# Seeding a PSUM bank with a ScalarE copy instead of summing two products on VectorE

## The chip, the cores and the metric

The kernel runs on one core of a Trainium2 chip. The metric is the device time of one execution in microseconds; the time before is 638.24 us, the median of three runs (637.68 to 638.25). Of one execution there is a profile, whose span is 636.4 us.

## The reference

The reference chains two blocks. The first is a state-space scan ("mamba2"): for 4 sequences of 768 tokens with 8 heads it works in chunks and gives, per token, 8 x 32 = 256 numbers. The second is a mixture of four experts over the resulting 3072 x 256 matrix:

```python
p = domain_probs / (domain_probs.sum(-1, keepdims=True) + 1e-09)
for e in range(E):
    h = np.maximum(x @ w1[e], 0.0)          # 256 -> 1024
    out += p[:, e:e + 1] * (h @ w2[e])      # 1024 -> 256
```

Everything is float32. The change concerns only the first product of an expert and its gate: `h = max(x @ w1, 0)`, scaled by the token's probability p.

## The kernel before

**Tiling.** The tokens come in 6 blocks of 512 (index k). For each block the kernel runs 8 steps (index r): 4 experts times 2 parts of the hidden layer. The steps are numbered n = 8k + r, from 0 to 47. Steps 0 and 1 are done plainly; steps 2 to 47 go through the loop at L820, and the change concerns only these.

**Seven products instead of eight.** In a step, both matrix products are done as 2 x 2 blocks by a Strassen-Winograd scheme: seven block products, of weights and tokens that were added up beforehand, take the place of eight. `fmul(n, i)`, L509 to L525, is the i-th product of the first layer: two matmul instructions of 128 x 256 in the program, each of which shows as two matmul records and two weight loads in the profile. `smul(n, i)`, L593 to L611, is the i-th product of the second layer, of the same size; it adds into the accumulators acc0 to acc3. In step n the loop mixes the `fmul` of step n with the `smul` of step n - 1, so that TensorE has work while VectorE and ScalarE prepare the hidden values of step n.

**Two banks of PSUM, X and Y.** The first layer's products go to two banks. X takes products 1, 6, 7 and 4, one added on the other. Y takes product 2 alone, and is then started again for products 5 and 3. The four blocks of the hidden layer are sums of these:

- block 11 = product 1 + product 2
- block 22 = products 1 + 6 + 7, plus product 5
- block 12 = products 1 + 6, plus products 5 + 3
- block 21 = products 1 + 6 + 7 + 4, which is X at the end

For the first three, X is needed at an intermediate stage. `snap(n, i)`, L527 to L530, is a ScalarE copy of X to SBUF after product i. `total(n, i, b)`, L532 to L535, is a VectorE sum of Y and that snapshot into a tile z. `gated(n, b, src)`, L537 to L547, is the VectorE instruction that takes the maximum with zero, multiplies by the gate p and writes the hidden block h; its source is z, or X for block 21. `diff`, L549 to L552, subtracts hidden blocks for the second layer.

**Order.** The schedule is written out by hand: each engine runs its instructions in the order of the program's text, and the framework only adds the semaphore waits. A step before the change begins so on TensorE: fmul 1 (X), fmul 2 (Y), smul(n-1, 1), fmul 6 (X), smul(n-1, 3), fmul 5 (Y), fmul 7 (X). On ScalarE it is snapshot 1, snapshot 6, snapshot 7; on VectorE it is the sum and the gate of block 11, then two late differences and attention work of the step before (`late`, `decay_part`, `combine`), then the sum and gate of block 22, and so on. Some steps also hold attention work: `masks` (ScalarE), `scores` (TensorE, steps with r = 3 and 6) and `outputs` (TensorE, r = 4 and 7). The scores of such a step borrow the banks X and Y at its end, and VectorE's masked products (L405) free them. `opened(n)`, L715 to L719, is the head of a step. `leave` issues the stores of a finished block on the DMA queue of SyncE.

**What waits on what, around the change.** fmul 6 adds to X, so it may run only after the snapshot of product 1 has been taken. fmul 5 restarts Y, so it may run only after the reader of product 2 in Y is done. A matmul with `start` set replaces what is in its bank; without it, it adds to what is there.

Of the kernel before, what the change touches and what calls it, by code (L numbers as in the profile page):

```python
# [8 lines left out]
FP32 = mybir.dt.float32  # L9
# [3 lines left out]
P = 128  # L13
# [4 lines left out]
def kernel(  # L18
# [38 lines left out]
    nc = tc.nc  # L57
# [6 lines left out]
    HB = BLK // 2  # L64
    CPB = BLK // P
# [6 lines left out]
    JJ = FH // HB  # L72
# [17 lines left out]
    ps_f = ctx.enter_context(tc.tile_pool(name="ps_f", bufs=1, space=bass.MemoryType.PSUM))  # L90
# [126 lines left out]
    for queue, c in ((nc.sync, slice(0, 1)), (nc.scalar, slice(1, SPREAD))):  # L217
        queue.dma_start(
            out=a_q.rearrange("(q r) c t s -> q r c (t s)", q=NQ)[:, 0, c],
            in_=a.rearrange("(i k) (q t) s -> k q i (t s)", k=NBLK, t=NT)[0][:, c])  # L220
# [4 lines left out]
        out=a_sb, in_=a.rearrange("c h s -> (c h) s").rearrange("(p r) s -> p r s", r=2))  # L225
# [147 lines left out]
    def masks(c):  # L373

        s = st[c]
        m = s["ctm"] = att.tile([HN, NT, P], FP32, tag="ctm", name="ctm")
        for t in range(NT):
            nc.scalar.mul(m[:, t], s["xb"][:, OCT:OCT + P], tmask[:, t:t + 1])
# [128 lines left out]
    first, hid, acc = {}, {}, {}  # L507

    def fmul(n, i):  # L509

        k = n // SPB
        f = first.setdefault(n, {})
        bank = "X" if i in (1, 6, 7, 4) else "Y"
        if i in (1, 2, 5):
            f[bank] = ps_f.tile([P, JJ, HB], FP32, tag=bank, name=bank)
        y, Y = yT[k], yS.get(k)
        w = (A11, A12, S4, A22, S1, S2, S3)[i - 1]
        b1, b2 = slice(0, HB), slice(HB, BLK)
        rhs = {1: y[:, 0, b1], 2: y[:, 1, b1], 3: y[:, 1, b2]}.get(i)
        if rhs is None:  # L520
            rhs = Y[:, {4: 3, 5: 0, 6: 1, 7: 2}[i]]
        for j in range(JJ):
            nc.tensor.matmul(  # L523
                out=f[bank][:, j], lhsT=wt1[n][:, w, j * P:j * P + P], rhs=rhs,
                start=(i in (1, 2, 5) and j == 0), stop=(j == JJ - 1), skip_group_check=True)  # L525

    def snap(n, i):  # L527

        s = first[n][i] = ffn.tile([P, JJ, HB], FP32, tag="snap", name="snap", bufs=4)
        nc.scalar.copy(out=s, in_=first[n]["X"])  # L530

    def total(n, i, b):  # L532

        z = first[n]["z" + b] = ffn.tile([P, JJ, HB], FP32, tag="z", name="z", bufs=3)
        nc.vector.tensor_add(z, first[n]["Y"], first[n][i])  # L535

    def gated(n, b, src):  # L537

        if n not in hid:
            hid[n] = {}  # L540
        h = hid[n][b] = ffn.tile([P, JJ, HB], FP32, tag="h" + b, name="h" + b)
        k, e = n // SPB, n % SPB // JJ
        half = int(b[1]) - 1
        g = gate[k, e].rearrange("p c s -> p (c s)")[:, half * HB:half * HB + HB]
        nc.vector.scalar_tensor_tensor(  # L545
            out=h, in0=first[n][src], scalar=0.0, in1=g.unsqueeze(1).to_broadcast([P, JJ, HB]),
            op0=ALU.max, op1=ALU.mult)  # L547
# [33 lines left out]
    def plain_second(n, b, d):  # L581


        k = n // SPB
        u, half = {(1, 1): (2, 1), (2, 1): (3, 0), (1, 2): (0, 1), (2, 2): (3, 1)}[d, b]
        begins = begin(k, u)
        for i, w in enumerate(((A11, A12), (S3, A22))[d - 1]):
            for j in range(JJ):
                nc.tensor.matmul(  # L589
                    out=acc[k, u][:, half], lhsT=w2_op(n, w)[:, j], rhs=hid[n][f"{i + 1}{b}"][:, j],  # L590
                    start=(begins and i == 0 and j == 0), stop=False, skip_group_check=True)

    def smul(n, i):  # L593

        if n < 0:
            return
        k = n // SPB
        if n < PLAIN:
            if n == PLAIN - 1 and i in (1, 7, 6, 4):
                m, d = divmod((1, 7, 6, 4).index(i), 2)  # L600
                plain_second(m, 2, d + 1)
            return
        u, half = divmod(ORDER.index(i), 2)
        begins = begin(k, u)
        w = (A11, A12, S4, A22, S1, S2, S3)[i - 1]
        rhs = hid[n][("11", "21", "22", "T4", "T1", "T2", "T3")[i - 1]]
        for j in range(JJ):
            nc.tensor.matmul(  # L608
                out=acc[k, u][:, half], lhsT=w2_op(n, w)[:, j], rhs=rhs[:, j],
                start=(begins and j == 0),  # L610
                stop=(n % SPB == SPB - 1 and j == JJ - 1), skip_group_check=True)  # L611
# [97 lines left out]
    def leave(k, c):  # L709

        for q in range(P // 32):
            for d in range(2):
                leave_part(k, c, q, d, nc.sync)

    def opened(n):  # L715

        fmul(n, 1)
        snap(n, 1)
        fmul(n, 2)  # L719


    homes = ((ps_s, "acc0"), (ps_s, "acc1"), (ps_att, "att"), (ps_att, "att"))
# [97 lines left out]
    for n in range(PLAIN, NS):  # L820
        k, r = divmod(n, SPB)

        ahead = CPB * (k + 1)
        scanned = [ahead + d for d in {0: [0], 2: [1], 4: [2], 5: [3]}.get(r, [])]
        scored = [ahead + d for d in {3: [0, 1], 6: [2, 3]}.get(r, [])]
        done = [ahead + d for d in {4: [0, 1], 7: [2, 3]}.get(r, [])]
        if k == NBLK - 1:
            scanned, scored, done = [], [], []
        ending = r == 0 and k > 0
        e = r // JJ  # L830
        if r % JJ == 0 and n + JJ < NS:
            load_gate(*divmod(n // JJ + 1, E))
        if PLAIN + 2 < n + 2 < NS:
            load_w1(n + 2)
            load_w2(n + 2)
        opened(n)
        total(n, 1, "11")
        gated(n, "11", "z11")
        behind = scored and k == 0
        last = behind and r == 6  # L840
        for work in late[:2] if behind else late:
            work()
        if r == 1 and k > 0:
            combine(k - 1, 0)
            combine(k - 1, 1)
        for c in scanned:
            decay_part(c, 0)
        for c in scored:
            masks(c)
        if k > 0 and 2 <= r < CPB + 2:  # L850
            leave(k - 1, r - 2)
        smul(n - 1, 1)
        fmul(n, 6)
        snap(n, 6)
        smul(n - 1, 3)
        if ending:
            keep(k - 1, 0)
        if done:
            outputs(done)
            states.extend(done)  # L860
        fmul(n, 5)
        fmul(n, 7)
        snap(n, 7)
        total(n, 7, "22")
        smul(n - 1, 7)
        smul(n - 1, 5)
        if ending:
            keep(k - 1, 1)
        gated(n, "22", "z22")
        if r == 1 and k > 0:  # L870
            combine(k - 1, 2)
        for c in scanned:
            decay_part(c, 1)
        for work in late[2:] if behind and not last else []:
            work()
        for c in scored if not last else []:
            decay_part(c, 2)
        if n == PLAIN:
            sum_w2(0, 1)
        elif n == SPB - 4:  # L880
            sum_w1(n + 2)
        elif n >= SPB - 3:
            sum_w2(n)
        if n < CPB:
            load_chunk(n + CPB)
        for c in scanned if n >= CPB else []:
            if c + 2 < NCH:
                load_decays(c + 2)
        for c in done:
            if c + CPB < NCH:  # L890
                load_tokens(c + CPB)
                load_heads(c + CPB)
        fmul(n, 3)
        total(n, 6, "12")
        fmul(n, 4)
        gated(n, "21", "X")
        for work in late[2:] if last else []:
            work()
        for c in scored if last else []:
            decay_part(c, 2)  # L900
        if not scored:
            gated(n, "12", "z12")
        if r == SPB - 1 and k < NBLK - 1:
            sums(k + 1)
        smul(n - 1, 6)
        if scored:
            scores(scored, ((ps_att, "att"), (ps_att, "att"), (ps_f, "Y"), (ps_f, "X")))
            masked(scored, (3, 2, 0, 1))
            gated(n, "12", "z12")
        smul(n - 1, 2)  # L910
        diff(n, "T3", "22", "12")
        smul(n - 1, 4)
        if n == PLAIN:
            sum_w2(1, 1)
        if n != SPB - 4:
            sum_w1(n + 2)
        if PLAIN < n < SPB - 4:
            sum_w2(n + 1)
        diff(n, "T1", "12", "11")
        if r == 1 and k > 0:  # L920
            turned_out(k - 1)
        late = [lambda n=n: diff(n, "T2", "22", "T1"), lambda n=n: diff(n, "T4", "21", "T2")]
        if states:
            late.append(lambda c=states.pop(0): carry(c))
# [48 lines left out]
```

## Time and profile before

| what | before |
|---|---|
| time, median of 3 runs | 638.24 us |
| span of the profiled execution | 636.4 us |
| TensorE busy | 631.9 us |
| VectorE busy | 483.4 us |
| ScalarE busy | 119.7 us |
| snapshots of X (L530) | 138, 586 ns each |
| sums of Y and a snapshot (L535) | 138, 686 ns each |
| gates that read z (L545) | 138, 724 ns each |
| gates that read X (L545) | 50, 684 ns each |

In the profile, PE is TensorE's matmul, PEld its weight load, DVE is VectorE, ACT is ScalarE and POOL is GpSimd. A row of the groups reads: line, engine, operation, output and input tile, shape, count, then the busy time and the mean of one in ns, then the idle time of the engine just ahead of these instructions and what ended it. A row of the timeline reads: start in us, length in us, engine, line, operation, count, and in brackets the idle time before it and what ended that. Matmul records overlap, so the length of a group of them is longer than the time it takes from the next one.

### The profile page before, as it was taken

To read this page: it belongs to the slowest core of one execution; us is meant where nothing else is said; L and a number is where in the kernel's file an instruction comes from. 1 tells how busy PE (TensorE), PEld (TensorE's weight loads), DVE (VectorE), ACT (ScalarE), POOL (GpSimd) and SP (SyncE) were. 2 spreads that over 40 slices of the span, in tenths; PEclk is the share of its full clock that TensorE was granted. 3 is DMA by queue.
4 is the path that set the end of the run, shared out by engine and by line. 5 is a ranking of instruction groups with operands and counts; after the bars stand their busy time and mean duration, and the time that the engine had idled before them with its cause. 6 is when DMAs were issued, how large, how long until landed. Compare 5 with 4: busy or idle time off the path is not lost.

```text
span 636.4 us, 9259 instructions
## 1 busy us (share of the span) xinstructions
PE 631.9 (99%) x3405; PEld 538.2 (85%) x3405; DVE 483.4 (76%) x810; ACT 119.7 (19%) x264; POOL 112.9 (18%) x164
## 2 busy tenths in 40 slices
PE   9999999999999999999999999999999999999997
PEld 5888888888888888888888888888888888888886
DVE  7868999887787788678687778778867677756555
ACT  4011221212111221122211221122111211111110
POOL 6788557020000002000002000000100000100001
PEclk9999999999999999999999999999999999999999
DMA  6998894745666392757284566639365644167001
GB/s 188 302 357 295 282 346 156 279 169 166 191 200 238 90 366 81 228 175 248 99 287 149 168 199 196 231 102 358 89 220 162 242 160 133 61 152 241 2 1 33
DMA packets 98513, 121.61 MB, mean 191 GB/s; under 512 B 29529, under 2 KB 81957, under 8 KB 98469
## 3 DMA queue, kind: packets, MB, share of 16 engines
q1 hardware_dynamic: 95512, 111.20, 53.7%
q0 software_dynamic: 2432, 9.50, 3.8%
q8 instruction: 27, 0.44, 0.3%
q10 hardware_dynamic: 524, 0.32, 0.2%
q14 instruction: 18, 0.14, 0.1%
HBM read 108.16 MB, written 12.83 MB: 190 GB/s over the span
## 4 chain that ended last, share of the span: by engine, by line
PE 99%; ACT 0%; DVE 0%; issue 0%
PE acc L608 44%; PE X L523 25%; PE Y L523 19%; PE acc L589 2%; PE g L393 2%; PE y L462 2%; PE X L572 1%; PE Y L572 1%; PE y L450 1%; PE t L729 1%; PE a L331 0%; PE y L428 0%; PE gp L309 0%; PE turned L655 0%; DVE o L686 0%; ACT p_sb L298 0%
## 5 line engine op out<-in xcount | busy, mean ns | idle before, releaser
L535 DVE TENSOR_TENSOR z<-Y,snap 128x512 f32<-128x512 f32 x138 | 94.6, 686 | 117.6 <-ACT snap L530 66.7
L608 PE MATMUL acc<-hT,wt 128*128 128x256 f32 x736 | 181.1, 379 | 0.0
L530 ACT COPY snap<-X 128x512 f32<-128x512 f32 x138 | 80.8, 586 | 464.2 <-PE X L523 403.5
L608 PEld LDWEIGHTS acc<-hT,wt 128*128 128x128 f32 x736 | 140.1, 190 | 18.7
L608 PE MATMUL acc<-h,wt 128*128 128x256 f32 x552 | 142.6, 381 | 0.0
L523 PE MATMUL X<-yS,wt 128*128 128x256 f32 x552 | 141.8, 380 | 0.0
L608 PEld LDWEIGHTS acc<-h,wt 128*128 128x128 f32 x552 | 104.2, 190 | 16.8 <-issue 2.3
L523 PEld LDWEIGHTS X<-yS,wt 128*128 128x128 f32 x552 | 105.0, 190 | 14.3 <-issue 0.3
L545 DVE SCALAR_TENSOR_TENSOR h<-z,gate 128x512 f32<-128x512 f32 x138 | 99.9, 724 | 3.5 <-PE acc L589 0.4
L523 PE MATMUL Y<-yT,wt 128*128 128x256 f32 x368 | 94.5, 379 | 0.0
L523 PEld LDWEIGHTS Y<-yT,wt 128*128 128x128 f32 x368 | 68.9, 190 | 10.5
L552 DVE TENSOR_TENSOR hT<-h,hT 128x512 f32<-128x512 f32 x92 | 65.2, 709 | 1.8
L552 DVE TENSOR_TENSOR hT<-h,h 128x512 f32<-128x512 f32 x92 | 65.1, 748 | 1.4
L364 DVE TENSOR_TENSOR_SCAN LT<-ab,ident 128x512 f32<-128x512 f32 x42 | 52.1, 1242 | 0.0
L523 PE MATMUL Y<-yS,wt 128*128 128x256 f32 x184 | 48.3, 385 | 0.0
L523 PE MATMUL X<-yT,wt 128*128 128x256 f32 x184 | 47.3, 379 | 0.0
L369 POOL TENSOR_TENSOR MT<-xb,LT 128x128 f32<-128x128 f32 x20 | 8.6, 428 | 205.4 <-PE Y L523 68.8
L405 DVE TENSOR_TENSOR MT<-g,LT 128x256 f32<-128x256 f32 x93 | 32.0, 415 | 11.5 <-PE g L393 11.4
L523 PEld LDWEIGHTS Y<-yS,wt 128*128 128x128 f32 x184 | 34.2, 190 | 6.4 <-issue 2.2
L523 PEld LDWEIGHTS X<-yT,wt 128*128 128x128 f32 x184 | 35.0, 190 | 4.7
L545 DVE SCALAR_TENSOR_TENSOR h<-X,gate 128x512 f32<-128x512 f32 x50 | 34.2, 684 | 5.0 <-PE X L523 3.4
L350 POOL TENSOR_TENSOR cts<-ctm,dec 128x256 f32<-128x256 f32 x20 | 14.1, 726 | 128.3 <-DVE dec L347 128.3
(103 smaller groups left out, 325.2 us busy)
## 6 DMA issues: line engine op xcount, KB each, us to landing
wt<-in_w_dram SPq DMA_DIRECT2D x112, 256.0 KB
wt<-w_d SPq DMA_DIRECT2D x40, 640.0 KB
wt<-w_d SPq DMA_DIRECT2D x40, 512.0 KB
ab<-acut_d SPq DMA_DIRECT2D x21, 512.0 KB
gate<-p_d SPq DMA_DIRECT2D x23, 256.0 KB
w_d<-wt POOLq DMA_DIRECT2D x8, 640.0 KB, 3.7
wt<-in_w_dram SPq DMA_DIRECT2D x40, 128.0 KB
w_d<-wt POOLq DMA_DIRECT2D x8, 512.0 KB, 7.7
```

Source lines behind the costliest of these rows:

```text
L350: nc.gpsimd.tensor_mul(cts, s["ctm"], dec.unsqueeze(1).to_broadcast([HN, NT, P]))
L364: nc.vector.tensor_tensor_scan(out=LT[:, i * w:i * w + w], data0=s["a"][i], data1=ident.rearrange("p h s -> p (h s)")[:, :w], initial=0.0, ...
L393: nc.tensor.matmul(out=g.rearrange("p t s -> p (t s)"), lhsT=s["xb"][k, OBT:OBT + P], rhs=s["ctm"][k].rearrange("p t s -> p (t s)"), start ...
L405: nc.vector.tensor_mul(s["MT"][:, h, 0:P], s["g"][q], s["LT"][:, h])
L462: nc.tensor.matmul(out=y[32 * q:32 * q + 32, t, 0:w], lhsT=s["xb"][:, h * D:h * D + D], rhs=s["MT"][:, NT * q + t, 0:w], start=(k == 0 and ...
L523: nc.tensor.matmul(out=f[bank][:, j], lhsT=wt1[n][:, w, j * P:j * P + P], rhs=rhs, start=(i in (1, 2, 5) and j == 0), stop=(j == JJ - 1), ...
L530: nc.scalar.copy(out=s, in_=first[n]["X"])
L535: nc.vector.tensor_add(z, first[n]["Y"], first[n][i])
L545: nc.vector.scalar_tensor_tensor(out=h, in0=first[n][src], scalar=0.0, in1=g.unsqueeze(1).to_broadcast([P, JJ, HB]), op0=ALU.max, op1=ALU. ...
L552: nc.vector.tensor_sub(h[o], h[x], h[y])
L572: nc.tensor.matmul(out=f[bank][:, j], lhsT=wt1[n][:, w, j * P:j * P + P], rhs=yT[k][:, i, cols], start=(i == 0 and j == 0), stop=(i == 1), ...
L608: nc.tensor.matmul(out=acc[k, u][:, half], lhsT=w2_op(n, w)[:, j], rhs=rhs[:, j], start=(begins and j == 0), stop=(n % SPB == SPB - 1 and ...
```

## The change

Product 1 is no longer snapshot to SBUF and added to product 2 on VectorE. Instead ScalarE copies bank X to bank Y, and product 2 is then added to that copy by TensorE itself, since its matmuls no longer start the bank afresh. VectorE's gate of block 11 then reads Y in PSUM directly. The sum for block 11 (one `total` in each of the 46 steps) is dropped. So that TensorE has something to do during the copy, smul(n-1, 1) is moved ahead of fmul 2, and a few lines that stand beside it (masks, stores) move with it. Its purpose is to take work from VectorE.

```diff
 def fmul(n, i):
-        if i in (1, 2, 5):
+        if i in (1, 5):
             f[bank] = ps_f.tile([P, JJ, HB], FP32, tag=bank, name=bank)
...
-                start=(i in (1, 2, 5) and j == 0), stop=(j == JJ - 1), skip_group_check=True)
+                start=(i in (1, 5) and j == 0), stop=(j == JJ - 1), skip_group_check=True)
...
 def opened(n):
         fmul(n, 1)
-        snap(n, 1)
-        fmul(n, 2)
+        first[n]["Y"] = ps_f.tile([P, JJ, HB], FP32, tag="Y", name="Y")
+        nc.scalar.copy(out=first[n]["Y"], in_=first[n]["X"])
...
         opened(n)
-        total(n, 1, "11")
-        gated(n, "11", "z11")
         behind = scored and k == 0
         last = behind and r == 6
+        for c in scored:
+            masks(c)
+        if k > 0 and 2 <= r < CPB + 2:
+            leave(k - 1, r - 2)
+        smul(n - 1, 1)
+        fmul(n, 2)
+        gated(n, "11", "Y")
         for work in late[:2] if behind else late:
             work()
...
         for c in scanned:
             decay_part(c, 0)
-        for c in scored:
-            masks(c)
-        if k > 0 and 2 <= r < CPB + 2:
-            leave(k - 1, r - 2)
-        smul(n - 1, 1)
         fmul(n, 6)
```

## The prediction

> **What bounds the kernel now.** I read the page first: busy time, then the chain that ended last.
>
> ```profile
> PE 631.9 (99%) x3405; PEld 538.2 (85%) x3405; DVE 483.4 (76%) x810; ACT 119.7 (19%) x264; POOL 112.9 (18%) x164
> ...
> PE 99%; ACT 0%; DVE 0%; issue 0%
> ```
>
> TensorE is busy 99% and is 99% of the chain. "Busy" alone could hide stalls, so I read the groups by shape and then one quiet step.
>
> ```profile
> L530 ACT COPY snap<-X 128x512 f32<-128x512 f32 x138 | 80.8, 586 | 464.2 <-PE X L523 403.5 <-DVE MT L405 60.8
> L535 DVE TENSOR_TENSOR z<-Y,snap 128x512 f32<-128x512 f32 x138 | 94.6, 686 | 117.6 <-ACT snap L530 66.7 <-PE Y L523 50.8
> L545 DVE SCALAR_TENSOR_TENSOR h<-z,gate 128x512 f32<-128x512 f32 x138 | 99.9, 724 | 3.5 <-PE acc L589 0.4
> ```
>
> These are the prices of what goes and of what replaces it: a copy out of PSUM 586 ns, a sum 686, a gate on the sum 724 (the gates that read X directly take 684 in a row beside it). VectorE waits for TensorE or for the copies, not the reverse. Now the head of a quiet step, in the timeline:
>
> ```profile
> 323.39 1.03 PE L523 MATMUL X<-yT,wt 128*128 128x256 f32 x4
> ...
> 324.04 0.84 PEld L523 LDWEIGHTS Y<-yT,wt 128*128 128x128 f32 x4
> 324.25 1.03 PE L523 MATMUL Y<-yT,wt 128*128 128x256 f32 x4
> 324.45 0.59 ACT L530 COPY snap<-X 128x512 f32<-128x512 f32 x1 [6.32 <-PE X L523]
> 324.90 0.84 PEld L608 LDWEIGHTS acc<-h,wt 128*128 128x128 f32 x4
> 325.12 1.03 PE L608 MATMUL acc<-h,wt 128*128 128x256 f32 x4
> ```
>
> A product (fmul or smul) is four matmul records. The next product starts 0.86 us after it (323.39, 324.25, 325.12), 0.216 each, though one record lasts 0.38. Each product's first weight load stands 0.21 us ahead of its first matmul. A quiet step has 14 products, 56 x 0.2158 = 12.09 us, and the trace has exactly 12.09 from step to step. So nothing can be gained in a quiet step; the longer steps (13.36, 13.9) hold the scores and outputs of the attention, whose small gaps come at changes of the matmul's shape, which the change doesn't touch.
>
> **What the Trainium skill says.**
> 1. "Perfetto Trace Analysis", Tensor Engine Instruction: the end of a matmul in a profile is computed, not observed, and matmul busy time is a bad metric. The trace agrees: 0.38 recorded against 0.216 of spacing. So I count by starts.
> 2. "TensorE: Matmul & The Clock Gate", Step-by-step: what each phase is for: the 64-deep window pulls weight loads ahead of running matmuls. The trace agrees (0.21 us ahead); this lead is what a late wait eats first.
> 3. "ScalarE: Activation LUTs", Step-by-step: what each stage is for: a ScalarE write to PSUM is faster than one to SBUF. No instruction here goes from PSUM to PSUM, so the trace is silent; prices below.
> 4. "PSUM — Partial Sum Buffer", The four PSUM rules: a matmul without the first-of-group mark adds onto what an engine wrote where an earlier matmul has marked the element. Every Y before it had such a matmul, so the trick needs no extra instruction.
>
> **The change part by part.** It applies to the 46 steps 2 to 47.
> Removed: 46 sums on VectorE (46 x 0.69 = 31.6 us) and the gate's read of z, which now reads Y in PSUM: 46 x 40 ns less, by the rows' 724 and 684. VectorE goes from 76% to about 71%. It is no part of the chain, so this is worth nothing by itself. It stays early enough for fmul 5, which restarts Y: after fmul 2 come fmul 6 and smul 3, 1.7 us, and the gate takes 0.1 + 0.69. In steps after scores, VectorE was free 1.08 us after fmul 2's end before; fmul 2 is now 0.86 later, so 0.22, and it still fits. The tightest later sum (fmul 7's, before fmul 3) had 0.25 us of idle time ahead of it; VectorE loses 0.79 us of work but TensorE reaches that point 0.86 earlier after fmul 2: 0.07 less slack, 0.18 left. Costed at nothing.
> Moved: smul(n-1, 1) before fmul 2, with inputs from the previous step, long ready. The masks and output stores stand ahead of it in program text, but on ScalarE and the store queue their order against their neighbours is the same. Nothing.
> Added: the copy X to Y takes the place of the snapshot, the same count and shape. The new thing is a wait on TensorE. Before, fmul 2 needed nothing from the copy, and its first reader on TensorE's side, fmul 6 (it writes X), came two products later. Now fmul 2 waits for the copy, with one product, smul(n-1, 1), to cover it; all of TensorE's queue stands behind it.
> In the lines above: the place of fmul 2's weight load becomes 324.90. The copy starts at 324.45 (37 ns after fmul 1's last recorded end, 36 to 37 in all 46 steps) and ends 585 ns later at 325.04, if it takes what a snapshot takes. The load then starts after a wake-up. So the load is late by 0.14 us plus the wake-up.
> How late may it be? Two places of this trace tell. Where fmul 3's load waits for the sum of fmul 7 it is 52 ns late, step after step, and its matmul is on time: small lateness is free. And step 2 has, once, just the new pattern (a copy covered by one product, as smul(1, 3) doesn't exist):
>
> ```profile
> 41.35 0.84 PEld L523 LDWEIGHTS Y<-yS,wt 128*128 128x128 f32 x4
> 41.56 1.03 PE L523 MATMUL Y<-yS,wt 128*128 128x256 f32 x4
> ...
> 41.77 0.58 ACT L530 COPY snap<-X 128x512 f32<-128x512 f32 x1 [2.87 <-PE X L523]
> 42.47 0.73 PEld L523 LDWEIGHTS X<-yS,wt 128*128 128x128 f32 x4 [0.28 <-issue]
> 42.49 1.10 PE L523 MATMUL X<-yS,wt 128*128 128x256 f32 x4
> 43.22 0.41 PEld L589 LDWEIGHTS acc<-h,wt 128*128 128x128 f32 x2
> 43.43 0.38 PE L589 MATMUL acc<-h,wt 128*128 128x256 f32 x1
> ```
>
> The load belongs at 41.35 + 0.86 = 42.21 and comes at 42.465, 251 ns late. From 41.56 to 43.43 lie two products, 1.87 us for 1.73: 143 ns lost. So 251 - 143 = 108 ns of lateness are free. (This load also passed a separate semaphore instruction, begun 38 ns after the copy's end and 51 long; fmul 2's wait for ScalarE is the last of its waits and should sit on the load itself.)
> With D the copy's duration and w the wake-up: lateness = 37 + D + w + 380 - 864 = D + w - 447 (380 is the last matmul's recorded length, 864 its start to the load's place); loss = D + w - 555, not below 0.
> w: 22 ns in the one load that waited directly for a ScalarE copy (at 9.04 us), 53 for loads after VectorE, 37 for the semaphore instruction. Range 22 to 50, I take 37.
> D: upper end 585, no gain from a PSUM target. Lower end: "Perfetto Trace Analysis", Optimizing Scalar/DVE Operations, gives ScalarE about 93 ns of access overhead on SBUF and 51 on PSUM, and the profiled latency about twice that: an estimate of 2 x 51 + 512 elements x 0.835 (the slope between this trace's copies of 256, 372 ns, and 512, 586) = 529. Between: writing to PSUM saves 93 - 51 = 42, or as much as reading from it saves, about 28 (186 for SBUF to SBUF by "ScalarE: Activation LUTs", What ACT_TABLE_LOAD costs, against 158 left of the 585 here). I take the middle, 35: D = 550.
> Loss: 550 + 37 - 555 = 32 ns in 45 steps (in step 2 two plain products cover the copy, 1.7 us): 1.44 us. Sum: 638.24 + 1.4 = 639.7 us.
>
> **The rivals.**
> A, the copy is just hidden: D + w at or below about 575, loss 0 to 20 ns, 638.2 to 639.1; typical D = 543, w = 22, 10 ns, 638.7, no change. For it: the free 108 ns and the skill on PSUM targets. Against: it needs both unknowns on their good side. This is the case "not slower".
> B, the PSUM target gains nothing or the wake-up is long: D = 585, w = 37 to 50, loss 67 to 80 ns, 3.0 to 3.6 us, 641.2 to 641.8. For it: all 138 snapshots take 585 to 590. Against: the skill's statement.
> C, the freed VectorE time removes stalls: for it only its 76%; against it, quiet steps without any stall, and step 2's 0.14 us as the sole stall at a buffer that I found. At most 0.3 us: 637.9.
>
> **How the numbers follow.** Forecast (loss 20 to 55 ns) 0.50; A 0.33; B 0.13; C 0.04. 0.2% is 1.28 us, 28 ns a step, inside the forecast's interval, so part of it counts as no change: faster 0.04, same 0.44, slower 0.52. The range leaves out B's far end and what lies below C: 637.9 to 641.5.
>
> **What would show it.** The row of copies Y<-X, 46 of them: its mean is D. In a quiet step, fmul 2's load should follow the copy's end by 22 to 50 ns, and the step should last 12.09 plus the loss, about 12.12; 12.09 proves A, over 12.15 proves B. The sums should number 92. Wrong altogether I'd be if copying from bank to bank ran at a slower rate per element, if the wait sat in a separate semaphore instruction (some 65 ns more), or if fmul 5 began to wait for the gate.

## The result

The changed kernel takes 640.89 us (median of four runs, 640.77 to 641.12) against 638.24: ratio 1.0045, 95% interval 1.003 to 1.0059. It is slower by 2.65 us, 0.4%; the prediction said 639.7, in 637.9 to 641.5.

The page of the changed kernel, in the parts shown of before:

```profile
PE 634.7 (99%) x3405; PEld 533.4 (83%) x3405; DVE 447.1 (70%) x764; ACT 119.0 (19%) x264; POOL 108.4 (17%) x164
...
PE 99%; ACT 0%; DVE 0%; issue 0%
...
L535 DVE TENSOR_TENSOR z<-Y,snap 128x512 f32<-128x512 f32 x92 | 62.9, 684 | 79.1 <-ACT snap L530 71.4
...
L545 DVE SCALAR_TENSOR_TENSOR h<-Y,gate 128x512 f32<-128x512 f32 x50 | 34.5, 691 | 80.3 <-PE Y L523 41.7
...
L719 ACT COPY Y<-X 128x512 f32<-128x512 f32 x46 | 26.2, 570 | 303.7 <-PE X L523 242.9
L523 PEld LDWEIGHTS Y<-yT,wt 128*128 128x128 f32 x368 | 65.1, 189 | 17.2 <-ACT Y L719 8.9
```

VectorE's 46 sums are gone and it is 36 us less busy, while TensorE's chain is still 99% of the span. The last row is the one to find: a weight load on Y, a thing that never waited for ScalarE before, now sits idle for 8.9 us behind the copy. That is idle time of the weight loads; the matmuls lose less, as the head of a step shows (timeline of the changed kernel, the step that was shown of before; the columns are start, length, engine and so on):

```profile
324.60 1.03 PE L523 MATMUL X<-yT,wt 128*128 128x256 f32 x4
...
325.25 0.84 PEld L608 LDWEIGHTS acc<-h,wt 128*128 128x128 f32 x4
325.47 1.03 PE L608 MATMUL acc<-h,wt 128*128 128x256 f32 x4
325.67 0.57 ACT L719 COPY Y<-X 128x512 f32<-128x512 f32 x1 [6.32 <-PE X L523]
326.29 0.73 PEld L523 LDWEIGHTS Y<-yT,wt 128*128 128x128 f32 x4 [0.20 <-ACT Y L719]
326.33 1.09 PE L523 MATMUL Y<-yT,wt 128*128 128x256 f32 x4
327.04 0.84 PEld L523 LDWEIGHTS X<-yS,wt 128*128 128x128 f32 x4
327.26 1.03 PE L523 MATMUL X<-yS,wt 128*128 128x256 f32 x4
```

The copy ends at 326.24 and the load of fmul 2 starts 52 ns later, 172 ns behind its place. fmul 2's first record still starts in its place (325.47 + 0.86 = 326.33); what is lost shows behind it: from fmul 2 (326.33) to fmul 6 (327.26) there are 0.93 us in place of 0.86. Taken to the nanosecond from the trace, each of the 45 steps from 3 to 47 loses 63 or 64 ns here, and a quiet step lasts 12.15 us in place of 12.09. 45 x 64 ns = 2.88 us; step 2 adds 0.10 (fmul 5 now waits for the gate there, 245 ns lost, where fmul 7 lost 142 before). From step 2 on, the two profiled runs differ by this sum, 2.98 us. The two spans differ by 2.8 (639.2 and 636.4), as the part ahead of step 2, the same program in both, was 0.23 us shorter in the profiled run of the changed kernel; it took 36.7 to 37.3 us in the profiled runs of this case. The medians differ by 2.65, with single runs of one kernel spread over 0.35 to 0.6.

### The profile page after: what moved, and what is told of

Same layout as the page of the kernel before. It is cut to its first block, busy times and chain, and to the rows that moved or that the text cites. A ratio compares the mean times of both kernels' runs of the same rounds, so it can differ in the third digit from the quotient of the medians.

```text
span 639.2 us, 9140 instructions
## 1 busy us (share of the span) xinstructions
PE 634.7 (99%) x3405; PEld 533.4 (83%) x3405; DVE 447.1 (70%) x764; ACT 119.0 (19%) x264; POOL 108.4 (17%) x164
## 4 chain that ended last, share of the span: by engine, by line
PE 99%; ACT 0%; DVE 0%; issue 0%
PE acc L608 44%; PE X L523 25%; PE Y L523 19%; PE acc L589 2%; PE g L393 2%; PE y L462 2%; PE X L572 1%; PE Y L572 1%; PE y L450 1%; PE t L729 1%; PE a L331 0%; PE y L428 0%; PE gp L309 0%; PE turned L655 0%; DVE o L686 0%; ACT p_sb L298 0%
## 5 line engine op out<-in xcount | busy, mean ns | idle before, releaser
L535 DVE TENSOR_TENSOR z<-Y,snap 128x512 f32<-128x512 f32 x92 | 62.9, 684 | 79.1 <-ACT snap L530 71.4
L523 PE MATMUL Y<-yT,wt 128*128 128x256 f32 x368 | 97.3, 387 | 0.0
L545 DVE SCALAR_TENSOR_TENSOR h<-Y,gate 128x512 f32<-128x512 f32 x50 | 34.5, 691 | 80.3 <-PE Y L523 41.7
L530 ACT COPY snap<-X 128x512 f32<-128x512 f32 x92 | 53.8, 585 | 165.0 <-PE X L523 165.0
L719 ACT COPY Y<-X 128x512 f32<-128x512 f32 x46 | 26.2, 570 | 303.7 <-PE X L523 242.9
L523 PEld LDWEIGHTS Y<-yT,wt 128*128 128x128 f32 x368 | 65.1, 189 | 17.2 <-ACT Y L719 8.9
L545 DVE SCALAR_TENSOR_TENSOR h<-z,gate 128x512 f32<-128x512 f32 x92 | 66.8, 726 | 1.9 <-PE acc L589 0.4
L552 DVE TENSOR_TENSOR hT<-h,h 128x512 f32<-128x512 f32 x92 | 63.8, 734 | 1.4
```

What stands on the lines that cost most here:

```text
L523: nc.tensor.matmul(out=f[bank][:, j], lhsT=wt1[n][:, w, j * P:j * P + P], rhs=rhs, start=(i in (1, 5) and j == 0), stop=(j == JJ - 1), ski ...
L545: nc.vector.scalar_tensor_tensor(out=h, in0=first[n][src], scalar=0.0, in1=g.unsqueeze(1).to_broadcast([P, JJ, HB]), op0=ALU.max, op1=ALU. ...
L552: nc.vector.tensor_sub(h[o], h[x], h[y])
L719: nc.scalar.copy(out=first[n]["Y"], in_=first[n]["X"])
```

## The experiments

The theory: fmul 2's load waits for the copy, 108 ns of its lateness cost nothing, and every nanosecond beyond is lost. A product that TensorE runs while the copy is made is called its cover. The rivals: the moved order of products costs the time; writing to PSUM, or adding onto a bank that ScalarE wrote, is slow in itself; VectorE's relief is a gain that the stall hides.

| kernel | time, us | ratio to before | 95% interval |
|---|---|---|---|
| changed kernel | 640.89 | 1.0045 | 1.003 to 1.0059 |
| moved order, sum kept | 642.18 | 1.0063 | 1.005 to 1.0076 |
| the same, scan later | 638.75 | 1.0009 | 1.0001 to 1.0017 |
| no copy | 638.33 | 1.0003 | 0.9995 to 1.0011 |
| no cover | 680.71 | 1.0667 | 1.0652 to 1.0682 |
| copy of 384 columns | 638.85 | 1.0009 | 1.0001 to 1.0017 |
| copy of 448 columns | 641.24 | 1.0046 | 1.0033 to 1.0059 |
| two products as cover | 640.23 | 1.0032 | 1.0019 to 1.0044 |
| two, but not behind scores | 639.90 | 1.0026 | 1.0016 to 1.0036 |
| two, mended | 638.35 | 1.0004 | 0.9996 to 1.0012 |

**No copy.** All edits of this part are against the changed kernel.

```diff
-        first[n]["Y"] = ps_f.tile([P, JJ, HB], FP32, tag="Y", name="Y")
-        nc.scalar.copy(out=first[n]["Y"], in_=first[n]["X"])
...
-        if i in (1, 5):
+        if i in (1, 2, 5):
...
-                start=(i in (1, 5) and j == 0), ...
+                start=(i in (1, 2, 5) and j == 0), ...
```

> The changed kernel without the copy: fmul 2 starts bank Y afresh, so product 1 is left out of block 11; order and VectorE's work are the changed kernel's, ScalarE has 46 copies less. Wait theory: the stall goes, and the 46 dropped sums bring nothing, 638.0 to 638.5 us. Rival, VectorE's relief is a gain that the stall hides: clearly under before, 636 to 637.5 us. Rival, order: 640.9 us.

638.33 us, no change. With the copy the whole loss goes, though the products are in the changed kernel's order, and 46 sums fewer on VectorE bring nothing that can be measured: the rival of a hidden gain falls.

**No cover.**

```diff
-        smul(n - 1, 1)
         fmul(n, 2)
         gated(n, "11", "Y")
+        smul(n - 1, 1)
```

> The changed kernel with fmul 2 directly behind fmul 1, so that no product covers the copy. Wait theory: the load of fmul 2 is late by 172 + 863 = 1035 ns, 108 of it free, 927 lost in each of 46 steps: 638.2 + 42.6 = 680.9 us. Rivals, order or slow bank: 641 to 643 us.

680.71 us. The timeline of one step of this kernel:

```profile
357.49 0.57 ACT L719 COPY Y<-X 128x512 f32<-128x512 f32 x1 [4.59 <-PE X L523]
358.11 0.73 PEld L523 LDWEIGHTS Y<-yT,wt 128*128 128x128 f32 x4 [1.06 <-ACT Y L719]
358.11 1.13 PE L523 MATMUL Y<-yT,wt 128*128 128x256 f32 x4 [0.66 <-ACT Y L719]
```

The load is 1036 ns late and the step loses 927, where 1035 and 927 were forecast with the 108 ns taken from one event of the kernel before. Note that the last row puts only 0.66 us down as PE's idle time, as the record of a matmul reaches past the start of the next; the count by starts is the one that adds up.

**A shorter copy.** The same program with less to copy; c is 384 or 448.

```diff
-        fmul(n, 1)
-        first[n]["Y"] = ps_f.tile([P, JJ, HB], FP32, tag="Y", name="Y")
-        nc.scalar.copy(out=first[n]["Y"], in_=first[n]["X"])
+        Y = first.setdefault(n, {})["Y"] = ps_f.tile([P, JJ, HB], FP32, tag="Y", name="Y")
+        nc.scalar.copy(out=Y.rearrange("p j m -> p (j m)"), in_=ident.rearrange("p h s -> p (h s)"))
+        fmul(n, 1)
+        nc.scalar.copy(
+            out=Y.rearrange("p j m -> p (j m)")[:, :c],
+            in_=first[n]["X"].rearrange("p j m -> p (j m)")[:, :c])
```

> The changed kernel with a copy of 384 of the 512 columns; ahead of fmul 1, ScalarE fills bank Y with a constant, so the last 128 columns of block 11 get that constant in place of product 1. Wait theory: the copy takes 570 - 128 x 0.833 = 463 ns, the load of fmul 2 is late by 37 + 463 + 52 + 380 - 864 = 68 ns, under the 108 that are free: no loss, 638.0 to 638.5 us. If the free lateness were nothing, 68 ns x 45 = 3.1 us over before less the 64 that the model takes off: 641.3 us. Rival, slow bank: 641 us or more, as there is one PSUM write more.

> The same with 448 columns; the last 64 columns of block 11 get the constant. Wait theory: the copy takes 517 ns, the load is late by 122 ns, 14 lost in each of 45 steps: 638.2 + 0.6 = 638.8 us. Rival, slow bank: 641 us or more.

638.85 and 641.24 us: both above the forecast. The copies took what was said, 463 and 517 ns. But they started 92 ns after fmul 1's last record instead of 37. A step of the kernel with 448 columns:

```profile
296.87 1.03 PE L523 MATMUL X<-yT,wt 128*128 128x256 f32 x4
...
297.99 0.52 ACT L720 COPY Y<-X 128x448 f32<-128x448 f32 x1 [2.53 <-PE X L523]
...
298.56 0.73 PEld L523 LDWEIGHTS Y<-yT,wt 128*128 128x128 f32 x4 [0.20 <-ACT Y L720]
298.60 1.09 PE L523 MATMUL Y<-yT,wt 128*128 128x256 f32 x4
```

From fmul 1's start to the copy's there are 1.12 us, where the changed kernel has 325.67 - 324.60 = 1.07. The copy has more than one wait in either kernel, and one of them sits in a separate semaphore instruction ahead of it. In the changed kernel that is the wait for VectorE, which outside step 2 is over at least 1.0 us before the copy starts; the wait for TensorE, which ends last, sits on the copy. Here the constant that fills Y puts a wait for ScalarE's own earlier write on the copy, and the wait for TensorE is the one in the separate instruction: 55 ns more. The expected lateness was wrong by 52 to 53 ns, nearly all of it this, and the loss at the lateness that came about is as the theory has it. The first point of the next table is fmul 3 of the kernel before, whose load belongs at 301.86 + 1.73 = 303.59 and whose matmuls start in their place, 302.08 + 1.73 = 303.81, within the rounding:

```profile
301.86 1.70 PEld L608 LDWEIGHTS acc<-hT,wt 128*128 128x128 f32 x8
302.08 1.89 PE L608 MATMUL acc<-hT,wt 128*128 128x256 f32 x8
...
303.64 0.79 PEld L523 LDWEIGHTS Y<-yT,wt 128*128 128x128 f32 x4
303.80 1.03 PE L523 MATMUL Y<-yT,wt 128*128 128x256 f32 x4
```

All the points together:

| where | load late by, ns | lost, ns |
|---|---|---|
| before, fmul 3 | 52 | 0 |
| copy of 384 columns | 121 | 12 |
| changed kernel | 172 | 64 |
| copy of 448 columns | 174 | 66 |
| before, step 2 | 251 | 142 |
| no cover | 1036 | 927 |

Loss is lateness less 108 or 109 in every row but the first, where the lateness is below that and nothing is lost. The copy of 448 columns loses as much as the whole copy though it moves less, so it is the time of arrival that counts. The rival of a slow bank falls with that: the 384-column kernel has one PSUM write more than the changed one in each step and is 2.0 us faster. The last kernel of this part, with the whole copy and no loss, shows the same.

**Moved order, sum kept.** The sum and the snapshot of before with the products' order of the changed kernel.

```diff
-        if i in (1, 5):
+        if i in (1, 2, 5):
...
-                start=(i in (1, 5) and j == 0), ...
+                start=(i in (1, 2, 5) and j == 0), ...
...
-        first[n]["Y"] = ps_f.tile([P, JJ, HB], FP32, tag="Y", name="Y")
-        nc.scalar.copy(out=first[n]["Y"], in_=first[n]["X"])
+        snap(n, 1)
...
-        gated(n, "11", "Y")
+        total(n, 1, "11")
+        gated(n, "11", "z11")
```

> The order of the products on TensorE is the changed kernel's (smul(n-1, 1) ahead of fmul 2, masks and stores moved), but product 1 is snapshot to SBUF and summed on VectorE as before, so fmul 2 doesn't wait for the copy. Wait theory (TensorE loses 64 ns a step because fmul 2 waits for a copy that one product covers): no loss, 638.0 to 638.5 us. Rival, the moved order costs the time: 640.9 us.

642.18 us: both the theory's number and the rival's were wrong. TensorE does not wait for the first snapshot here. The timeline of one of the steps that got longer, from fmul 7 to fmul 3:

```profile
187.26 1.03 PE L523 MATMUL X<-yS,wt 128*128 128x256 f32 x4
...
188.12 1.89 PE L608 MATMUL acc<-hT,wt 128*128 128x256 f32 x8
...
188.32 0.59 ACT L530 COPY snap<-X 128x512 f32<-128x512 f32 x1 [2.00 <-PE X L523]
188.34 1.22 DVE L364 TENSOR_TENSOR_SCAN LT<-ab,ident 128x512 f32<-128x512 f32 x1
189.47 0.67 DVE L535 TENSOR_TENSOR z<-Y,snap 128x512 f32<-128x512 f32 x1
190.17 0.69 DVE L545 SCALAR_TENSOR_TENSOR h<-z,gate 128x512 f32<-128x512 f32 x1
190.19 0.73 PEld L523 LDWEIGHTS Y<-yT,wt 128*128 128x128 f32 x4 [0.58 <-DVE z L535]
190.19 1.13 PE L523 MATMUL Y<-yT,wt 128*128 128x256 f32 x4 [0.18 <-DVE z L535]
```

Snapshot 7 is ready at 188.91, but VectorE is still in the decay scan until about 189.5, and the sum that fmul 3 waits for comes late. fmul 2 comes one product later in this order, so VectorE's block of sum, gate, differences, carry and scan starts 0.86 us later, while fmul 7 does not move. Before, VectorE had 0.25 us to spare in these steps. The stall is 0.445 us in each of eight steps (r = 5 and r = 0, where a carry and a scan fall together), 3.6 us; step 2 has 0.3 more than before and step 6 0.1, together the 4.0 that are measured. To see whether this is all of it, the scan was moved:

```diff
-        for c in scanned:
-            decay_part(c, 0)
         fmul(n, 6)
...
         for c in scanned:
+            decay_part(c, 0)
             decay_part(c, 1)
```

> The version with the moved order and the VectorE sum kept (642.18 us), with the first decay scan of a step (1.22 us on VectorE) moved from behind block 11's gate to behind block 22's. Theory, its 4 us come from VectorE being late for the sum of fmul 7 that fmul 3 waits for: this wait goes, 638.2 to 639.2 us, if the later sums stay in time. Rival, the moved products cost by themselves on TensorE: still 642 us.

638.75 us. The eight stalls are gone, and 0.56 us are left in step 6, where the sum is now late behind other work. So the moved order costs nothing on TensorE itself; with the sum kept and the scan in its old place it costs 4 us, because VectorE comes late. The dropped sum is what pays for it: with it dropped, VectorE has 0.11 to 0.13 us left ahead of that sum in those same steps of the changed kernel.

**Two products as cover.**

```diff
-    late = []
+    late, held = [], []
...
+        if held:
+            smul(held.pop(), 4)
         smul(n - 1, 1)
         fmul(n, 2)
...
-        smul(n - 1, 4)
+        held.append(n - 1)
...
+    smul(held.pop(), 4)
```

> The changed kernel with smul(n-2, 4) held back from the end of the step before and put between fmul 1 and smul(n-1, 1), so that two products cover the copy. Wait theory: fmul 2's weight load is no longer late (172 ns less 863), the 2.9 us come back, 638.0 to 638.5 us; in the ten steps after scores, bank X may come free late for fmul 1, which could leave up to 1 us: at most 639.2. Rival, writing to PSUM from ScalarE or adding onto such a bank is itself slow: still 640.9 us.

> smul(n-2, 4) is held back only behind steps without scores; behind the ten steps with scores it stays where it was, and one product covers the copy. Wait theory: 64 ns lost in 10 of 45 steps, 638.2 + 0.6 = 638.8 us; below the version that always holds it back only if bank X is late there. Rival, slow bank: 640.9 us.

640.23 and 639.90 us, both 1 us or more above the forecast. The load of fmul 2 is on time wherever two products cover the copy (lateness 0), as forecast. The rest was in places that the forecast had left out. In both, the last product of step 1 is held back past the point where GpSimd has rewritten its weights, so it uses other weights (this is the part of the computation that these two change). Step 3 of the first kernel:

```profile
48.80 0.73 PEld L523 LDWEIGHTS X<-yT,wt 128*128 128x128 f32 x4 [0.32 <-DVE h L545]
...
50.46 0.73 PEld L589 LDWEIGHTS acc<-h,wt 128*128 128x128 f32 x4 [0.93 <-POOL wt L193]
```

The held product waits for GpSimd, 0.79 us lost, and fmul 1, which now comes earlier, waits for VectorE's gate to free bank X, 0.19 lost: 0.98 us in all. In the first, fmul 1 also waits for bank X after scores, 0.1 us in most of these steps and 0.2 in step 7. The second has instead ten stalls of 64 ns. With 0.1 in step 2: 0.98 + 1.1 + 0.1 = 2.2 and 0.98 + 0.64 + 0.1 = 1.7 us, against measured 2.0 and 1.7. The mended version keeps out of these places:

```diff
+        if held:
+            smul(held.pop(), 4)
         smul(n - 1, 1)
+        if done:
+            smul(n - 1, 3)
         fmul(n, 2)
...
-        smul(n - 1, 3)
+        if not done:
+            smul(n - 1, 3)
...
-        smul(n - 1, 4)
+        if scored or n == PLAIN:
+            smul(n - 1, 4)
+        else:
+            held.append(n - 1)
```

> The changed kernel with two products between fmul 1 and fmul 2 in every step but 2 and 3, without the losses of the two earlier versions: smul(n-2, 4) is held back only behind steps without scores and not behind step 2; in the ten steps after scores, smul(n-1, 3) is put ahead of fmul 2 instead (there the attention outputs lie between snapshot 6 and fmul 7). Wait theory: fmul 2's load is nowhere late but in step 3 (64 ns); step 2 keeps the 0.1 us more than before that the changed kernel has: 638.2 + 0.2 = 638.4 us, no gain over before. Rival, VectorE's relief is worth something once the stall is gone: under 637.5 us.

638.35 us, as expected. The head of a step of this kernel, with two products on acc between fmul 1 and fmul 2:

```profile
553.27 1.03 PE L608 MATMUL acc<-hT,wt 128*128 128x256 f32 x4
553.48 0.57 ACT L719 COPY Y<-X 128x512 f32<-128x512 f32 x1 [5.46 <-PE X L523]
...
554.14 1.03 PE L608 MATMUL acc<-h,wt 128*128 128x256 f32 x4
554.79 0.84 PEld L523 LDWEIGHTS Y<-yT,wt 128*128 128x128 f32 x4
555.00 1.03 PE L523 MATMUL Y<-yT,wt 128*128 128x256 f32 x4
...
555.87 0.81 PE L523 MATMUL X<-yS,wt 128*128 128x256 f32 x3
```

The copy ends at 554.05, 0.74 us ahead of the load, and the products follow each other every 0.86 us. This is the change without its stall, and it equals the kernel before within the interval: neither version beats it. Here fmul 2 adds onto what ScalarE wrote and takes 0.86 to 0.87 us (555.00 to 555.87) like every product, so the adding costs no time that shows.

## Why the prediction was right, point by point

- **The bound.** Right: quiet steps had no gap, TensorE's chain is 99% before and after, and 36 us less of VectorE bring nothing (no copy: 638.33).
- **The wait.** Right: in 45 steps fmul 2's load waits for the copy, the wait sits on the load itself, and the copy starts 37 ns after fmul 1's last record. Step 2 is the exception: there only fmul 6 lies between fmul 2 and fmul 5, as smul(1, 3) doesn't exist, and fmul 5 does wait for the gate, which the prediction had named among the signs of being wrong. It happens in this one step and adds 0.10 us; there is no other new stall.
- **The free 108 ns.** Right, and now shown over six points from 52 to 1036 ns: the one below 108 loses nothing, the others what lies beyond.
- **The size.** Off by half: the sum was 45 x 32 ns = 1.44 us; it is 45 x 64 = 2.88. Two terms were too small. D, the copy's time, is 570 ns: a PSUM target saves 15 ns against the 585 of a copy to SBUF, where I took 35, the middle of 28 and 42; the 28 compared a page's 186 ns, whose memories the page does not name, with the 158 here. The Trainium skill is right that PSUM is the faster target ("ScalarE: Activation LUTs", Step-by-step: what each stage is for); the overheads of "Perfetto Trace Analysis" (Optimizing Scalar/DVE Operations), from which I worked out 529 as the lower end, don't give this copy's time. w, the wake-up, is 51 to 52 ns: the value for loads that wait for VectorE (53) was the right neighbour, and the one load after ScalarE with 22, of another shape, was not typical; the range of 22 to 50 had left the 53 out. With the measured terms the formula D + w - 555 gives 67; 64 was lost. Of the 3 ns between, two come from its constants: for its 380 and 864 the trace has 379 and 865 in this place.
- **The rivals.** A (hidden) needed D + w of 575 at most; it is 622. B with 67 ns upward is nearly what came; I had given it 0.13 and the interval below it (20 to 55 ns) 0.50, and 64 lies between. The range held because it reached up into B, to 641.5, not because the favoured case came: that is in part luck. A quiet step lasts 12.15 us, where 12.12 was expected and more than 12.15 was to prove B. C (VectorE's relief gains) is ruled out as far as can be measured by the kernel without the copy.
- **The slack of VectorE.** 0.18 us was forecast ahead of the sum of fmul 7; 0.11 to 0.13 is measured. It held, but "costed at nothing" for the move stands only together with the dropped sum: by itself the move costs 4 us, which I had not seen.

## What to carry to other kernels

Where one engine has no gaps, as here, work taken from its neighbours is worth nothing, and a new wait on it is worth counting in nanoseconds: place of the load, end of the producer, wake-up, less the lead that the load has. A copy that must come between two dependent products wants more cover than its own length. Here 37 + 570 + 52 = 659 ns stood against a cover of one product, 0.86 us, less the 0.16 by which fmul 1's last record outlasts its spacing, less the load's lead of 0.21, plus the 0.11 that are free: 0.60. And a reordering on one engine shifts what the next engine can do when: look at the in-order queue of that engine before calling a move free.

## What the runs showed of the hardware that was not expected

- A ScalarE copy from PSUM to PSUM of 128 x 512 float32 took 570 ns in all 46 cases, 448 columns 517 and 384 columns 463, so 0.83 to 0.84 ns per column; the snapshots of the same size to SBUF took 585 to 590.
- In this row of products a weight load 52 ns late cost nothing, and one 121 to 1036 ns late cost its lateness less 108 or 109, though a load is 190 ns long. Its usual lead over its matmul is 213 to 215 ns, so about half of that sufficed.
- It mattered which of a copy's waits sat in the separate semaphore instruction ahead of it. With VectorE's wait there, long over, the copy started 37 ns after the matmul's recorded end; with TensorE's wait there, which ended last, 92 ns after it.
